# A hand-made issue order built anew: other keys for every step, and three more margins in the planner

## The chip, the cores and the metric

One core of one Trainium2 chip runs the kernel. The metric is the device time of one execution in microseconds (us). TensorE is called PE, its weight loads PEld, VectorE DVE, ScalarE ACT, GpSimd POOL; SyncE (SP) issues nearly all DMAs, and its queue is SPq in the profile.

## What is computed

A causal seven-tap local average with softmax weights, then a two-layer block with SoLU and a normalization in between (cut from the reference):

```python
# x (8, 4160, 192), weight_gen (8, 4160, 8 heads, 7 taps)
w = exp(weight_gen - max); w = w / (sum(w) + 1e-09)
out = einsum('bshk,bskhg->bshg', w, x_unf)        # x_unf: 7 shifted copies of x, zeros ahead
x = out.reshape(33280, 192)
h = x @ w_in                                      # 192 x 1024
e = exp(h - max(h)); sm = e / (sum(e) + 1e-09)
solu = h * sm
ln = (solu - mean) / sqrt(var + 1e-06) * g_ln
return ln @ w_out                                 # 1024 x 192
```

## The kernel before

The 33280 rows are cut into 260 tiles of 128 rows (128 partitions hold runs of 260 consecutive rows; tile t is row t of each run). Sixteen tiles make a chunk (the first two are 4 and 8 tiles), four tiles a group. Numbers are split into two float16 halves ("high" and "low"), so each product is three matmuls with the halves.

The work of a tile is a chain of steps over the five engines. The names in brackets are those of the planner.

- Per chunk: SP loads x in four parts (`lx0` to `lx3`, L87) and the weights (`lw`, L93); seven steps make the softmax of the taps (`t0` to `t6`; `t5` is DVE's reciprocal on L122, `t6` POOL's multiplication on L124); ACT and DVE compute the scale of the chunk (`v0` to `v5`).
- Per group of four tiles: POOL multiplies x by the taps (`attA`, L180) and adds part of the seven products (`attB`, L195). In two groups of four DVE adds the rest (`fin`, L458, tile `a`); in the other two PE adds them while it transposes. POOL has three buffers `pr`.
- Per pair of tiles: PE transposes the pair into PSUM tile `pa` (`xT`, L474: nine matmuls from `pr`, or three from `a`); ACT takes the high half (`xhi`, L484), DVE the low one (`xld`, L488) into `xh`; SP copies 64 partitions of `xh` to the other half of the partitions, both ways, into `turned` (`sw`, L494, two DMAs: the exchange of halves). `xh` and `turned` have four buffers each.
- Per tile: PE's first product (`mm1`, L508 and L513, twelve matmuls into `h`) reads `xh` and `turned`. Then DVE `max` (L525), ACT `exp` (L531), DVE `solu` (L539), ACT `sq` (L545) and `hi` (L552), DVE `lo` (L556). `h` has three buffers, so `mm1` of tile t waits for `sq` and `lo` of tile t - 3. SP transposes both halves by DMA (`tr`, L564) into `hlT` (six buffers, so it waits for `mm2` of tile t - 6). PE's second product (`mm2`, L604, 24 matmuls) follows, then ACT `out` (L615), and once in four tiles SP stores (`od`, L618). Small steps `f0` to `f5` per group make the normalization's scales.

Every engine runs its instructions in the order in which the program gives them. That order is not the source's: `plan` lists each step with its engine, a cost in ns and the steps it follows, and `issue_order` runs a list scheduling over it. When an engine comes free in that model, it takes, of the steps that are ready by then, the one with the smallest key. The key is the tile number plus an entry of the table `URGENCY`; an entry such as `mm1_3` is for that tile alone, `mm1` for all others. `gap` says how long after a step its follower counts as ready; `MARGIN`, looked up by the first two letters of both names, adds nanoseconds to it for tiles above 11. Nothing of the model reaches the chip but the order: on the chip an instruction starts when its inputs are there and the ones ahead of it on its engine have been issued.

```python
key = [round(t + URGENCY.get(f"{name}_{t}", URGENCY.get(name, 0)), 6) for name, t, *_ in steps]
...
    late = MARGIN.get((step[0][:2], to[0][:2]), 0) if to[1] > 11 else 0
...
    name, t, _, cost, *_ = steps[i]
    order.append((name, t))
```

Of the kernel before, what the change touches and what calls it, by code (L numbers as in the profile page):

```python
# [26 lines left out]
def tile_kernel(ctx: ExitStack, tc: tile.TileContext, x, weight_gen, w_in, w_out, g_ln, out):  # L27
# [642 lines left out]


URGENCY = dict(
    a00=71.5, a01=199.3, a02=-74.3, a03=-138.9, a04=-169.6, a10=-89.4, a11=203.9, a12=90.1,
    a13=-52.8, a14=90.6, attA=102.4, attA_0=57.6, attA_2=16.5, attA_4=-68.2, attA_6=-48.8,
    attA_8=83, attB=119.3, attB_0=-211.7, attB_2=5.7, attB_4=41.6, attB_6=-32, attB_8=-5.3,
    b0=239.2, b1=12.3, b2=-212.2, b3=-146.2, b4=171.8, c00=84.4, c01=55, c02=-166.7, c10=20.3,
    c11=135.4, c12=117.8, c20=-32.3, c21=-46.1, c22=-89, c30=95.7, c31=-78.4, c32=-191, dup=57.3,
    dup_0=0.9, dup_2=-49.2, dup_4=18.3, dup_6=109.3, dup_8=-102.8, exp=-176.9, exp_0=75.9,
    exp_1=-2.7, exp_10=179.6, exp_11=-117.4, exp_2=-0.5, exp_3=-46.2, exp_4=-188, exp_5=-32.6,
    exp_6=-150.7, exp_7=-98.5, exp_8=-221.2, exp_9=-48.7, f0=-122.4, f0_1=54.1, f0_11=-81.6,  # L680
    f0_3=79.3, f0_5=-73.5, f0_7=-51.7, f1=-185.9, f1_1=209.6, f1_11=162.5, f1_3=-185.1, f1_5=14.2,
    f1_7=118.9, f2=-25.5, f2_1=140, f2_11=-3.2, f2_3=76.2, f2_5=37.3, f2_7=-21.4, f3=95.6,
    f3_1=142.7, f3_11=86.8, f3_3=-147.3, f3_5=-184.5, f3_7=-139.5, f4=-147.9, f4_1=35.8,
    f4_11=-213.2, f4_3=156.3, f4_5=-57.7, f4_7=162.9, f5=-70.1, f5_1=-10.5, f5_11=-124.5,
    f5_3=-15.6, f5_5=-48.4, f5_7=-152.3, fin=188.2, hi=37.5, hi_0=148.8, hi_1=-28.1, hi_10=-47.9,
    hi_11=52.9, hi_2=45, hi_3=-174.9, hi_4=98.5, hi_5=44.4, hi_6=-12.5, hi_7=-111.8, hi_8=177.4,
    hi_9=0.2, lo=-185.7, lo_0=-96.1, lo_1=168, lo_10=83.3, lo_11=112.6, lo_2=43, lo_3=-9.3,
    lo_4=-94.3, lo_5=-69.3, lo_6=-100.4, lo_7=-194.9, lo_8=231.8, lo_9=-61.3, lw=-84.8, lx0=-101.7,
    lx1=-64.2, lx2=-78.8, lx3=-37.7, max=97.3, max_0=-15.2, max_1=-102.4, max_10=-26.9,
    max_11=-14.8, max_2=-40.5, max_3=-197.3, max_4=18.4, max_5=-82.8, max_6=-206.8, max_7=-49.1,  # L690
    max_8=27.3, max_9=-25.4, mm1=-18.1, mm1_0=-24.2, mm1_1=-1.2, mm1_10=-64.4, mm1_11=-47.7,
    mm1_2=173.8, mm1_3=91.2, mm1_4=31.9, mm1_5=-39.6, mm1_6=-0.8, mm1_7=30.6, mm1_8=27.5765,
    mm1_9=-213.6, mm2=-11.4, mm2_0=-133.1, mm2_1=-31.1, mm2_10=108.3, mm2_11=197.9, mm2_2=-56.1,
    mm2_3=-73.5, mm2_4=85.6, mm2_5=14.1, mm2_6=-97.8, mm2_7=-39.3, mm2_8=18.4, mm2_9=58.5, n0=-90.7,
    n1=-39.4, n2=-116, n3=-82.1, n4=-83.6, n5=-87.1, n6=-56.8, n7=-63, nq=-111.6, od=-162.9,
    od_11=-14.1, od_3=81.1, od_7=-146.5, out=-240.4, out_0=-17.5, out_1=0.12526, out_10=18.9,
    out_11=50.9, out_2=-92.8, out_3=-21.1, out_4=219.7, out_5=-76.7, out_6=-65.5, out_7=36.3,
    out_8=-199.4, out_9=-127.6, p30=-243.7, p31=-6.2, p4=78.6, p5=-112.5, p6=78.6, p70=208.1,
    p71=-151, p80=-114, p81=-169.3, p9=74, q00=-231.7, q01=-7.3, q02=146, q10=-178.8, q11=85,
    q12=-209.5, q20=22.2, q21=4.2, q22=-232.2, q30=151, q31=-39.3, q32=67.5, solu=-164.3,  # L700
    solu_0=-104.7, solu_1=-50.5, solu_10=238.5, solu_11=80.8, solu_2=210.1, solu_3=-56.1,
    solu_4=144.2, solu_5=-5.7, solu_6=103.5, solu_7=193.1, solu_8=96.9, solu_9=-154.4, sq=94.8,
    sq_0=73.6, sq_1=114.8, sq_10=-8.4, sq_11=166.9, sq_2=-191.8, sq_3=100.9, sq_4=79.7, sq_5=-175.5,
    sq_6=87.2, sq_7=231, sq_8=-43.1, sq_9=15.3, sw=-10.8, sw_0=14.2, sw_10=-0.6, sw_2=-85.8,
    sw_4=11.9, sw_6=-101.3, sw_8=-70.3, t0=243.9, t0_0=-146.7, t0_4=187.5, t1=28.4, t1_0=-142.4,
    t1_4=60.2, t2=70.4, t2_0=56.7, t2_4=204.6, t3=189.9, t3_0=148.2, t3_4=-233.9, t4=99.7,
    t4_0=-99.3, t4_4=93.5, t5=226.6, t5_0=84.6, t5_4=103.6, t6=44.7, t6_0=147.6, t6_4=30, tr=124.8,
    tr_0=-73, tr_1=186.1, tr_10=81.7, tr_11=135.8, tr_2=134.6, tr_3=-158.7, tr_4=-171.4, tr_5=89.1,
    tr_6=33.7, tr_7=31, tr_8=148.1, tr_9=-215.3, v00=-156.7, v00_0=-71.2, v00_4=129.8, v01=130.6,
    v01_0=124.8, v01_4=18.5, v02=163.5, v03=89.6, v1=-101.5, v1_0=-175.6, v1_4=62.2, v2=61.2,  # L710
    v2_0=67.1, v2_4=-138.4, v3=193.6, v3_0=86, v3_4=165.3, v4=-59.5, v4_0=-225.6, v4_4=-229.6,
    v5=-1.5, v5_0=59.8, v5_4=56.8, w0=-14.1, w1=-65.5, x0=50, x1=-101.8, xT=-20.7, xT_0=-130.6,
    xT_10=224.8, xT_2=-144.6, xT_4=-175.2, xT_6=-66.3, xT_8=157.5, xhi=-136.6, xhi_0=-227.5,
    xhi_10=238.1, xhi_2=27.4, xhi_4=-213.7, xhi_6=44, xhi_8=-195.5, xld=105.4, xld_0=129.3,
# [211 lines left out]
def held(t):  # L926
# [114 lines left out]
```

## Time and profile before

| | |
|---|---|
| time, median of 3 runs (lowest to highest) | 1304.97 us (1304.77 to 1308.33) |
| the profiled execution: its time | 1307.43 us |
| its span, first to last instruction | 1305.4 us |
| mean granted PE clock | 0.979 |
| busy: PE, DVE, POOL, ACT | 92%, 89%, 88%, 87% |
| HBM read and written | 46.19 MB, 25.56 MB |

No engine is full on average, and four of them are between 87% and 92% busy. The work of 16 tiles repeats from about 146 us to 1142 us; ahead of it the weights are prepared and the pipeline fills, behind it the last tiles drain and no softmax work is left. The stretch from 146.2 to 1141.7 us is 13 such cycles, measured from the first product of tile 20 to that of tile 228. In a cycle PE issues 32 products (16 `mm1` and 16 `mm2`) and eight `xT`.

### The profile page before, as it was taken

What the parts mean: (1) busy time and instruction counts of PE and PEld (TensorE: products, weight loads), DVE (VectorE), ACT (ScalarE), POOL (GpSimd) and SP (SyncE); (2) the same over time, 40 slices, a digit from 0 to 9 for tenths busy, and PEclk for the clock granted to TensorE, in tenths of its full rate; (3) what the DMA queues carried; (4) which work ended last, traced back from release to release, by engine and by line L of the source; (5) the groups of instructions that cost most, each with busy time, mean ns of one, the idle gap of its engine ahead of it and who ended that gap; (6) DMA issues with size and microseconds to landing.
All of it is one profiled execution on the core that took longest, in us unless ns stands there. A gap on an engine that the chain in (4) does not pass through costs nothing.

```text
span 1305.4 us, 27349 instructions
## 1 busy us (share of the span) xinstructions
PE 1206.9 (92%) x10248; PEld 822.9 (63%) x10248; DVE 1157.8 (89%) x1786; ACT 1137.1 (87%) x2311; POOL 1146.7 (88%) x237
## 2 busy tenths in 40 slices
PE   2698999989999998989899999999999999999998
PEld 2364666656666665656666566666666666666666
DVE  6778889979899997989989899999989899999894
ACT  5788979878898988989888898989899898998886
POOL 4999999988989999798997989899899989999700
PEclk9799999989999998999999999999999999999999
DMA  6578688777878878697987979889797989977686
GB/s 211 139 182 181 132 177 173 166 159 151 200 157 193 179 161 179 134 197 157 192 154 149 209 144 200 166 175 184 156 208 143 206 157 183 169 152 127 138 167 128
DMA packets 586066, 219.75 MB, mean 168 GB/s; under 512 B 548687, under 2 KB 566223, under 8 KB 585806
## 3 DMA queue, kind: packets, MB, share of 16 engines
q1 hardware_dynamic: 585632, 216.91, 79.9%
q8 instruction: 80, 1.31, 0.4%
q10 hardware_dynamic: 302, 1.11, 0.3%
q14 instruction: 52, 0.43, 0.1%
HBM read 46.19 MB, written 25.56 MB: 55 GB/s over the span
## 4 chain that ended last, share of the span: by engine, by line
PE 39%; ACT 25%; DVE 17%; issue 10%; DMA 6%; SPq 2%; ACTq 0%; DVEq 0%
PE po L604 15%; PE h L513 13%; PE h L508 7%; ACT e L531 7%; ACT e L545 6%; DVE h L525 5%; DVE h L539 5%; ACT hl L552 5%; DMA turned<-xh 4%; DVE hl L556 3%; PE pa L474 3%; ACT ot L615 2%; DVE a L458 2%; ACT junk L145 2%; ACT xh L484 1%
## 5 line engine op out<-in xcount | busy, mean ns | idle before, releaser
L180 POOL TENSOR_TENSOR pr<-xt,wt 128x5376 f32<-128x5376 f32 (+1 forms) x67 | 631.1, 9419 | 4.6 <-PE pa L474 4.3
L604 PE MATMUL po<-w_hl,hlT 128*128 128x192 f16 x6192 | 557.4, 247 | 4.1 <-ACT ot L615 3.5
L604 PEld LDWEIGHTS <-hlT 128*128 128x128 f16 x6240 | 526.7, 98 | 45.4 <-issue 9.5
L195 POOL TENSOR_TENSOR pr<-pr 128x2304 f32<-128x2304 f32 (+1 forms) x126 | 457.9, 3634 | 8.8
L525 DVE TENSOR_SCALAR_CACHE_REDUCE h<-h,row 128x1024 f32<-128x1024 f32 x260 | 334.8, 1288 | 66.0 <-PE h L513 65.3
L539 DVE SCALAR_TENSOR_TENSOR h<-h,row,e 128x1024 f32<-128x1024 f32 x260 | 334.6, 1287 | 23.0 <-ACT e L531 20.3
L531 ACT ACTIVATE e<-h,stats 128x1024 f32<-128x1024 f32 x260 | 291.6, 1122 | 56.8 <-DVE h L525 54.1
L556 DVE SCALAR_TENSOR_TENSOR hl<-h,hl 128x1024 f16<-128x1024 f32 x260 | 315.8, 1220 | 24.3 <-ACT e L545 16.2
L552 ACT ACTIVATE hl<-h 128x1024 f16<-128x1024 f32 x260 | 266.3, 1025 | 40.7 <-DVE h L539 25.1
L545 ACT ACTIVATE e<-h,stats 128x1024 f32<-128x1024 f32 x260 | 290.5, 1118 | 4.0 <-DVE h L539 1.9
L513 PEld LDWEIGHTS <-xh 128*128 128x128 f16 x1560 | 133.4, 99 | 242.4 <-issue 124.1
L513 PE MATMUL h<-w_odd,xh 128*128 128x512 f16 x780 | 192.6, 383 | 0.0
L513 PE MATMUL h<-wa_hi,xh 128*128 128x512 f16 x520 | 183.8, 395 | 0.0
L508 PE MATMUL h<-wb_hi,turned 64*128 64x512 f16 x260 | 102.4, 394 | 40.2 <-DMA turned<-xh 40.1
L615 ACT ACTIVATE ot<-po,stats 128x192 f32<-128x192 f32 x258 | 109.3, 423 | 14.9 <-PE po L604 14.8
L508 PE MATMUL h<-w_odd,turned 64*128 64x512 f16 x390 | 106.7, 380 | 12.5 <-ACT e L545 8.8
L508 PE MATMUL h<-wb_hi,xh 64*128 64x512 f16 x260 | 101.2, 389 | 12.6 <-DVE stats L576 8.8
L508 PEld LDWEIGHTS <-turned 64*128 64x128 f16 x780 | 55.0, 95 | 89.3 <-DMA turned<-xh 45.9
L508 PE MATMUL h<-w_odd,xh 64*128 64x512 f16 x390 | 106.9, 381 | 0.0
L513 PE MATMUL h<-wa_lo,xh 128*128 128x512 f16 x260 | 102.5, 394 | 0.0
L474 PE MATMUL pa<-ident,pr 128*128 128x128 f32 x678 | 87.1, 276 | 3.5 <-DVE xh L488 3.5
L474 PEld LDWEIGHTS pa<-ident,pr 128*128 128x128 f32 x678 | 79.3, 143 | 15.3 <-issue 3.5
(89 smaller groups left out, 1011.7 us busy)
## 6 DMA issues: line engine op xcount, KB each, us to landing
out_dram<-ot SPq DMA_DIRECT2D x65, 384.0 KB, 3.2
xt<-in_x_dram SPq DMA_DIRECT2D x30, 576.0 KB, 4.8
xt<-in_x_dram SPq DMA_DIRECT2D x30, 480.0 KB, 4.1
turned<-xh SPq DMA_DIRECT2D x260, 32.0 KB, 2.1
wt<-in_weight_gen_dram SPq DMA_DIRECT2D x15, 448.0 KB, 4.7
hlT<-hl SPq DMA_TRANSPOSE x260, 4.6
xt<-in_x_dram SPq DMA_DIRECT2D x3, 384.0 KB, 4.7
pr<-in_moe_w_out_dram SPq DMA_DIRECT2D x1, 1024.0 KB, 10.1
```

Of the source, the lines that this page charges most:

```text
L180: nc.gpsimd.tensor_tensor(out=window(pr, 0, [(ROW, K), (HG, n * H), (1, HG)]), in0=window(xt, t * D, [(D, K), (HG, n * H), (1, HG)]), in1= ...
L195: nc.gpsimd.tensor_tensor(out=b, in0=b, in1=a, op=ALU.add)
L474: nc.tensor.matmul(pa[:, k], source[:, first : first + P], ident, is_transpose=True, start=at == 0, stop=at == 3 * len(sources) - 1,)
L508: nc.tensor.matmul(h[:, fs], last[(f + odd) % 2][rows, low], rhs[rows], start=n == 0, stop=False)
L513: nc.tensor.matmul(h[:, fs], xh[:, 2 * odd, low], rhs[:, fs], start=False, stop=n == 2)
L525: nc.vector.tensor_scalar(h, h, row(t, BACK), 3.0e38, op0=ALU.mult, op1=ALU.min, accum_out=stat(t, NMAX))
L531: nc.scalar.activation(e, h_of[t], AF.Exp, bias=stat(t, NMAX), scale=-1.0, accum_out=stat(t, Z))
L539: nc.vector.scalar_tensor_tensor(out=h, in0=h, scalar=row(t, SCALE), in1=e, op0=ALU.mult, op1=ALU.mult, accum_out=stat(t, M))
L545: nc.scalar.activation(e_of.pop(t), h_of[t], AF.Square, bias=stat(t, M), scale=-float(FF), accum_out=stat(t, Q),)
L552: nc.scalar.activation(hl[:, 0, :], h_of[t], AF.Copy, scale=2.0**14)
L556: nc.vector.scalar_tensor_tensor(out=hl[:, 1, :], in0=h_of[t], scalar=2.0**14, in1=hl[:, 0, :], op0=ALU.mult, op1=ALU.subtract,)
L604: nc.tensor.matmul(po[:, :D], hlT[:, half * NJ + j, :], w2_hl[:, j, w, :], start=n == 0, stop=n == len(terms) - 1,)
```

## The change

Nearly every entry of `URGENCY` has another value, and `MARGIN` has three entries more: `sw` to `mm1` (and any other name with these first letters) 6000 ns, `xld` to `sw` 1500 ns, `mm2` to `tr` 1000 ns. `plan`, the costs, the buffers and the steps themselves stay. Of the table, one line of each side:

```diff
-    b0=239.2, b1=12.3, b2=-212.2, b3=-146.2, b4=171.8, c00=84.4, c01=55, c02=-166.7, c10=20.3,
+    attA=42.9, attA_0=-139.3, attA_2=38.7, attA_4=-121.9, attA_6=101.7, attA_8=-218.2,
...
 MARGIN = {
     ("lx", "v0"): 6000, ("lw", "t0"): 6000, ("lx", "at"): 6000, ("t0", "t1"): 6000,
     ("t1", "t2"): 3000, ("t2", "t3"): 3000, ("t3", "t4"): 3000, ("v2", "t4"): 3000,
-    ("t5", "t6"): 6000,
+    ("t5", "t6"): 6000, ("sw", "mm"): 6000, ("xl", "sw"): 1500, ("mm", "tr"): 1000,
 }
```

**SP, around the store of tiles 140 to 143** (the row `out_0_dram<-ot`). Before, the two exchanges here are those of tiles 152 and 154, and the transposing DMA in the first row is that of tile 146:

```order
L564 DMA_TRANSPOSE hlT_9359<-hl_9334 128x16x128
L564 DMA_TRANSPOSE hlT_9414<-hl_9388 128x16x128
L494 DMA turned_9482<-xh_9454 64x256 x2
L564 DMA_TRANSPOSE hlT_9488<-hl_9462 128x16x128
L618 DMA out_0_dram<-ot_9284 128x768
L564 DMA_TRANSPOSE hlT_9581<-hl_9518 128x16x128
L564 DMA_TRANSPOSE hlT_9605<-hl_9584 128x16x128
L494 DMA turned_9633<-xh_9578 64x256 x2
```

After, around the same store; the first transposing DMA is that of tile 144, and the exchanges are again those of tiles 152 and 154, with that of tile 156 in the last row:

```order
L564 DMA_TRANSPOSE hlT_9269<-hl_9230 128x16x128
L564 DMA_TRANSPOSE hlT_9328<-hl_9302 128x16x128
L494 DMA turned_9331<-xh_9262 64x256 x2
L564 DMA_TRANSPOSE hlT_9380<-hl_9345 128x16x128
L494 DMA turned_9405<-xh_9372 64x256 x2
L564 DMA_TRANSPOSE hlT_9453<-hl_9403 128x16x128
L618 DMA out_0_dram<-ot_9323 128x768
L564 DMA_TRANSPOSE hlT_9538<-hl_9484 128x16x128
L564 DMA_TRANSPOSE hlT_9593<-hl_9560 128x16x128
L87 DMA xt_9600<-in_x_dram 128x960
L93 DMA wt_9615<-in_weight_gen_dram 128x896
L494 DMA turned_9655<-xh_9562 64x256 x2
```

The exchange of tile 152 stood behind the transposing DMA of tile 147 and now stands behind that of tile 145; that of tile 154 moved from behind tile 150's to behind tile 146's.

**DVE, around `fin` of tile 156** (the row L458). Before, it follows the maximum of tile 150:

```order
L488 TENSOR_TENSOR xh_9454<-pa_9416,xh_9454 128x3x128
L556 SCALAR_TENSOR_TENSOR hl_9462<-h_9339,hl_9462 128x1024
L539 SCALAR_TENSOR_TENSOR h_9392,stats_135<-h_9392,row_8248,e_9466 128x1024
L525 TENSOR_SCALAR h_9468,stats_135<-h_9468,row_8248 128x1024
L458 TENSOR_REDUCE a_9521<-pr_9281 128x768
L556 SCALAR_TENSOR_TENSOR hl_9518<-h_9392,hl_9518 128x1024
```

After, it follows the maximum of tile 149 and a small step of the scales:

```order
L525 TENSOR_SCALAR h_9438,stats_135<-h_9438,row_8094 128x1024
L576 TENSOR_REDUCE stats_135<-stats_135 128x4
L458 TENSOR_REDUCE a_9492<-pr_9228 128x768
L556 SCALAR_TENSOR_TENSOR hl_9484<-h_9382,hl_9484 128x1024
L539 SCALAR_TENSOR_TENSOR h_9438,stats_135<-h_9438,row_8094,e_9508 128x1024
```

The addition comes one tile of DVE's work earlier.

**POOL, around `t6` of the chunk that starts at tile 164** (the row L124). Before:

```order
L180 TENSOR_TENSOR pr_11235<-xt_9659,wt_8682 128x5376
L195 TENSOR_TENSOR pr_11235<-pr_11235 128x2304
L195 TENSOR_TENSOR pr_11235<-pr_11235 128x768
L124 TENSOR_TENSOR wt_9661<-wt_9661,wy_10643 128x896
L180 TENSOR_TENSOR pr_11481<-xt_9659,wt_8682 128x5376
```

After:

```order
L180 TENSOR_TENSOR pr_11186<-xt_9600,wt_8636 128x5376
L124 TENSOR_TENSOR wt_9615<-wt_9615,wy_10380 128x896
L195 TENSOR_TENSOR pr_11186<-pr_11186 128x2304
L195 TENSOR_TENSOR pr_11186<-pr_11186 128x768
L180 TENSOR_TENSOR pr_11445<-xt_9600,wt_8636 128x5376
```

The multiplication that reads DVE's reciprocal now stands ahead of the group's additions instead of behind them.

## Rows read from the trace of the kernel before

**Rows 1.** Busy time by stretch: engines in their order, then granted clock, DMA share, GB/s.

```profile
core 0: us, PE busy (x) PEld busy (x) DVE busy (x) ACT busy (x) POOL busy (x), PEclk, DMA share, GB/s
0.00:146.20 146.20, 100.91 (x727) 66.01 (x728) 111.49 (x185) 112.99 (x257) 126.97 (x37) 0.92 0.70 171
146.20:1141.70 995.50, 950.85 (x8137) 647.27 (x8136) 908.82 (x1392) 889.69 (x1796) 931.24 (x184) 0.98 0.84 172
...
842.60:917.70 75.10, 72.06 (x625) 49.31 (x624) 69.81 (x108) 68.31 (x139) 71.60 (x15) 1.00 0.88 177
```

**Rows 2.** What PE waited for from 146.2 to 1141.7: total us, times, longest.

```profile
PE h L508 <- DMA turned<-xh: 36.5, 15, 5.9
PE h L508 <- ACT e L545: 5.8, 13, 0.6
PE h L508 <- DVE hl L556: 1.3, 2, 0.7
PE po L604 <- ACT ot L615: 0.9, 2, 0.7
```

**Rows 3.** The first of these waits over the whole span.

```profile
PE h L508 <- DMA turned<-xh: 40.1, 17, 5.9
```

**Rows 4.** Timeline of one stop, tile 188: start us, us, engine, line, operation.

```profile
946.72 0.55 DVE L488 TENSOR_TENSOR xh<-pa,xh 128x384 f16<-128x384 f32 x1
...
948.81 4.37 SPq L564 DMA_TRANSPOSE hlT<-hl  x1
...
953.28 1.18 SPq L494 DMA_DIRECT2D turned<-xh  x2
...
953.41 0.39 PE L508 MATMUL h<-wb_hi,xh 64*128 64x512 f16 x1
...
956.17 0.39 PE L508 MATMUL h<-wb_hi,turned 64*128 64x512 f16 x1 [2.38 <-DMA turned<-xh]
```

**Rows 5.** All uses of tile `turned`: from a DMA's issue to its landing.

```profile
DMA to landing us min/median/max: 1.7/2.1/6.3
```

**Rows 6.** What POOL waited for from 146.2 to 1141.7.

```profile
POOL wt L124 <- DVE wy L122: 52.6, 12, 7.0
POOL pr L180 <- PE pa L474: 4.3, 1, 4.3
```

**Rows 7.** The same in its four last cycles, 842.6 to 1141.7.

```profile
POOL wt L124 <- DVE wy L122: 12.6, 4, 3.4
```

**Rows 8.** Timeline of POOL around the end of tiles 184's and 180's groups.

```profile
877.13 8.57 POOL L195 TENSOR_TENSOR pr<-pr 128x2304 f32<-128x2304 f32 x2
...
895.43 6.97 POOL L195 TENSOR_TENSOR pr<-pr 128x2304 f32<-128x2304 f32 x2
```

**Rows 9.** Timeline of PE: the transposes of tiles 180 (from `a`) and 184 (from `pr`).

```profile
906.18 0.49 PE L474 MATMUL pa<-ident,a 128*128 128x128 f32 x3
...
923.90 1.15 PE L474 MATMUL pa<-ident,pr 128*128 128x128 f32 x9
```

**Rows 10.** Timeline of DVE: `fin` of tile 180.

```profile
898.16 1.78 DVE L458 TENSOR_REDUCE a<-pr 128x768 f32<-128x1536 f32 x1
```

**Rows 11.** Busy time by stretch again, a slow cycle.

```profile
612.60:691.20 78.60, 74.80 (x627) 50.61 (x628) 69.86 (x108) 68.59 (x139) 71.20 (x14) 0.96 0.86 168
```

More of the change, by code (lines that the diff above doesn't have):

```diff
@@ L672 @@
 URGENCY = dict(
-    a00=71.5, a01=199.3, a02=-74.3, a03=-138.9, a04=-169.6, a10=-89.4, a11=203.9, a12=90.1,
-    a13=-52.8, a14=90.6, attA=102.4, attA_0=57.6, attA_2=16.5, attA_4=-68.2, attA_6=-48.8,
-    attA_8=83, attB=119.3, attB_0=-211.7, attB_2=5.7, attB_4=41.6, attB_6=-32, attB_8=-5.3,
-    b0=239.2, b1=12.3, b2=-212.2, b3=-146.2, b4=171.8, c00=84.4, c01=55, c02=-166.7, c10=20.3,
-    c11=135.4, c12=117.8, c20=-32.3, c21=-46.1, c22=-89, c30=95.7, c31=-78.4, c32=-191, dup=57.3,
-    dup_0=0.9, dup_2=-49.2, dup_4=18.3, dup_6=109.3, dup_8=-102.8, exp=-176.9, exp_0=75.9,
@@ L679 @@
[L679 to L714, printed above, removed]
@@ L715 @@
-    xld_10=-17.8, xld_2=8.82093, xld_4=198.6, xld_6=23.9, xld_8=-2.6,
+    a00=79.1, a01=227.6, a02=-179.6, a03=77, a04=-12.8, a10=2, a11=-93.6, a12=123.9, a13=124.9,
+    a14=-132.6, attA=42.9, attA_0=-139.3, attA_2=38.7, attA_4=-121.9, attA_6=101.7, attA_8=-218.2,
+    attB=39.9, attB_0=-162.5, attB_2=-4.3, attB_4=74.8, attB_6=-6.9, attB_8=38, b0=133.1, b1=124.8,
+    b2=-185.2, b3=24.4, b4=6.5, c00=-95.6, c01=-188.7, c02=-219.3, c10=-222.3, c11=130.7, c12=-70.5,
+    c20=-32.3, c21=-46.1, c22=-89, c30=95.7, c31=-78.4, c32=-191, dup=57.3, dup_0=0.9, dup_2=-49.2,
@@ new lines @@
+    dup_4=18.3, dup_6=109.3, dup_8=-102.8, exp=-62.2, exp_0=-133.3, exp_1=-123.8, exp_10=41,
+    exp_11=-48.7, exp_2=130, exp_3=117.3, exp_4=-23.5, exp_5=-229.6, exp_6=143.2, exp_7=-6.5,
+    exp_8=-204.3, exp_9=-18.4, f0=-44.8, f0_1=204, f0_11=72.8, f0_3=17.5, f0_5=17.9, f0_7=216.7,
+    f1=-76, f1_1=20.8, f1_11=-49, f1_3=225.5, f1_5=239.7, f1_7=-14.9, f2=-157.8, f2_1=-115.4,
+    f2_11=-19.4, f2_3=230.5, f2_5=-82.5, f2_7=-212.3, f3=34.7, f3_1=-22.7, f3_11=-9.5, f3_3=-53.7,
+    f3_5=-121.9, f3_7=-4.3, f4=-58.5, f4_1=167.1, f4_11=69.9, f4_3=-149.7, f4_5=-211.4, f4_7=-100.7,
@@ new lines @@
+    f5=-113, f5_1=-19.9, f5_11=23.1, f5_3=75.1, f5_5=47.8, f5_7=96.3, fin=117.5, hi=-107.7,
+    hi_0=83.5, hi_1=117.9, hi_10=-193.7, hi_11=86.1, hi_2=-36.8, hi_3=165.8, hi_4=-85.5, hi_5=32.6,
+    hi_6=-10, hi_7=-26.8, hi_8=154.8, hi_9=166, lo=-80.2, lo_0=57.7, lo_1=-5.6, lo_10=102.5,
+    lo_11=-17.3765, lo_2=-76.7, lo_3=23.7, lo_4=164.3, lo_5=95.8, lo_6=-169.7, lo_7=50, lo_8=-126.6,
+    lo_9=75, lw=235.7, lx0=-56.1, lx1=92.4, lx2=8.2, lx3=54.9, max=202.4, max_0=-105.2, max_1=98.3,
+    max_10=233.7, max_11=125.3, max_2=-23.8, max_3=200.8, max_4=-205, max_5=-32.1, max_6=149.3,
@@ new lines @@
+    max_7=-60.8, max_8=-133.6, max_9=-98.2, mm1=-25.2, mm1_0=-8.9, mm1_1=-9.6, mm1_10=239.3,
+    mm1_11=96.5, mm1_2=158.9, mm1_3=48.1, mm1_4=130.2, mm1_5=-233.5, mm1_6=-5.2, mm1_7=-0.8,
+    mm1_8=-2.4, mm1_9=50.4, mm2=-18.3, mm2_0=-4.1, mm2_1=-79.4, mm2_10=182.9, mm2_11=-132.6,
+    mm2_2=-211.7, mm2_3=118.1, mm2_4=-93, mm2_5=-224.9, mm2_6=147, mm2_7=10.4, mm2_8=71.6,
+    mm2_9=96.2, n0=-12.3, n1=122.3, n2=213.8, n3=-82.1, n4=-104.5, n5=-87.1, n6=-157.4, n7=-151.2,
+    nq=-111.6, od=-89.4, od_11=20.6, od_3=16.1, od_7=25.3, out=-192.5, out_0=82.9, out_1=-156.2,
@@ new lines @@
+    out_10=54, out_11=-146.8, out_2=232.1, out_3=-56.4, out_4=-28.7, out_5=6.1, out_6=-127.6,
+    out_7=23.7, out_8=-74.6, out_9=81.9, p30=-18.7, p31=-152.9, p4=235.2, p5=33.4, p6=-71.9,
+    p70=197.2, p71=64.7, p80=-220.6, p81=-108.5, p9=116.9, q00=125.4, q01=-132, q02=161.9,
+    q10=219.6, q11=-64, q12=-61.2, q20=206.5, q21=-15.5, q22=-201.1, q30=39.3, q31=0.6, q32=-134.4,
+    solu=125.9, solu_0=20.8, solu_1=-3.5, solu_10=129.7, solu_11=17.6, solu_2=6.1, solu_3=-139.9,
+    solu_4=-75.7, solu_5=-145.2, solu_6=161.6, solu_7=-195.9, solu_8=-29.1, solu_9=37.3, sq=-43.8,
@@ new lines @@
+    sq_0=215.3, sq_1=24.9, sq_10=40.3, sq_11=25.5, sq_2=-12.8, sq_3=-12.2, sq_4=105.1, sq_5=-121,
+    sq_6=213.5, sq_7=195, sq_8=12.2, sq_9=135, sw=-185.3, sw_0=13.8, sw_10=20.2, sw_2=-59.6,
+    sw_4=-155.5, sw_6=-182.2, sw_8=175, t0=212.4, t0_0=-187, t0_4=28.8, t1=140.8, t1_0=-28.9,
+    t1_4=183.2, t2=-37.7, t2_0=-126.3, t2_4=-82.2, t3=-76.5, t3_0=-74.6, t3_4=38.2, t4=-62.6,
+    t4_0=-136.6, t4_4=-54.8, t5=-63.4, t5_0=-21.5, t5_4=76, t6=-177.7, t6_0=-127.1, t6_4=6.6,
+    tr=92.3, tr_0=149.1, tr_1=51.9, tr_10=240.9, tr_11=-11.4, tr_2=116.2, tr_3=181, tr_4=-86.1,
@@ new lines @@
+    tr_5=-53, tr_6=80.2, tr_7=-115.4, tr_8=-93.9, tr_9=-198.8, v00=-59.2, v00_0=115.8, v00_4=5.3,
+    v01=-39.3, v01_0=223.2, v01_4=-36.3, v02=168.3, v03=-45.4, v1=222.8, v1_0=15.8, v1_4=1.3,
+    v2=-79.9, v2_0=202.6, v2_4=206.9, v3=194.4, v3_0=-66.4, v3_4=3.8, v4=47.2, v4_0=49.8,
+    v4_4=-37.3, v5=115.1, v5_0=-200.7, v5_4=75.3, w0=12.4, w1=-58.5, x0=115.8, x1=-0.7, xT=-175.2,
+    xT_0=-80.4, xT_10=-88.9, xT_2=57.7, xT_4=-138, xT_6=-69.7, xT_8=245, xhi=-93.7, xhi_0=-188.9,
+    xhi_10=-138.1, xhi_2=19.7, xhi_4=-3.8, xhi_6=24.9, xhi_8=178.1, xld=249.2, xld_0=-95.4,
@@ L716 @@
+    xld_10=99.8, xld_2=-77.8, xld_4=-238.1, xld_6=8.8, xld_8=133.1,
 )
```

## The prediction

> **What bounds the kernel now.** I read the busy time by stretch first. From 146.2 to 1141.7 us the work of 16 tiles repeats 13 times in 995.5 us, 76.6 us a cycle, and PE is busy for 950.9 us of it, more than any other engine [rows 1]. In a cycle where PE's clock was 1.00 throughout, its work is 72.06 us [rows 1], so 13 cycles need 936.8 us; the other 14.1 us of PE's busy time are time at the lower of its two clock levels (1.2 and 2.4 GHz, the stretch's mean is 0.98). Next I read what PE waited for in this stretch: 36.5 us for `turned`, 5.8 us for ACT's squares, 1.3 us for DVE's low half, 0.9 us for ACT's `out`, 44.5 us in all [rows 2]. Busy time and waits add up to the 995.5 us, so PE is the bound, and 58.6 us (44.5 and 14.1) is all that an order could take from this stretch without shortening PE's work.
>
> The largest wait has one cause that the timeline shows. DVE finished the low half of tile 188 at 947.27 us. SP issued its exchange at 953.28 us: until 953.18 its queue was in a transposing DMA that took 4.37 us to issue. PE had begun that tile's first product at 953.41, and stood until the halves had landed, at 956.17 [rows 4]. So it is the place in SP's queue, not the length of the transfer, that makes PE stop.
>
> **The exchange, part one of the change.** Counted in the written order over tiles 20 to 249, 2.61 products of PE lie on average between an exchange and the product that needs it before, and 8.83 after. A cycle has 32 products, so one stands for 72.06 / 32 = 2.25 us, its share of the transposes included; the lead goes from 5.9 to 19.9 us. The longest stop of PE at `turned` is 5.9 us [rows 3] and a landing takes at most 6.3 us [rows 5]; both together stay below the new lead. I take all 36.5 us of the stretch out, and the 40.1 - 36.5 = 3.6 us ahead of and behind it [rows 2, 3]. With the stops goes what follows them: the lowered clock. Nearly all of PE's waiting is for `turned`, the other waits being at most 0.7 us long [rows 2], so I give it all 14.1 us back. Together **54.2 us**. The exchange itself does the same two DMAs; what moves with it costs nothing as long as SP's queue is not fuller, and it holds the same DMAs as before.
>
> Here a rule of the Trainium skill speaks against any gain. The page "DMA: Bandwidth & Descriptors", section "Anatomy of one DMA — SWDGE (gpsimd) path", gives a fixed cost of about 2.0 us plus the bytes over 436 GB/s, for another issuing path than SP's. By that a copy of 32 KB would take an estimated 2.1 us, the old lead would have covered it, and there would be no wait to remove. The median landing agrees with the page, 2.1 us [rows 5]; the timeline does not agree that the lead was there, since the copy was issued just ahead of the product [rows 4].
>
> **The transposes of x move with it.** To be exchanged earlier a pair has to be transposed earlier: `xT` stands 11.80 products ahead of `mm1` instead of 5.30, that is 6.5 x 2.25 = 14.6 us. Who is late next? POOL finished the group of tile 184 at 902.4 us [rows 8], and PE transposed it at 923.9 [rows 9]: 21.5 us of lead, of which 6.9 remain. In the groups that DVE finishes, POOL was done at 885.7 us [rows 8], and PE transposed at 906.2 [rows 9]; `fin` took 1.78 us of these 20.5 [rows 10], so 20.5 - 1.8 - 14.6 = 4.1 us remain, if DVE takes `fin` up as early as the new order has it (1.48 products ahead of `xT`, before 3.79). Both are covered, so I cost the move at nothing; without that cover each microsecond that POOL or DVE comes later would be one of PE's. A buffer bounds the move too: `xh` and `turned` hold four pairs, and the new order starts a pair 11.80 products, about six tiles, ahead, which leaves one tile. The cast and the subtraction of a pair move along on ACT and DVE; there are as many as before, and what their new places do to the tiles' own steps is in the term of ACT and DVE below.
>
> **The margin ahead of the transposing DMAs, and SP.** `mm2` to `tr` puts these DMAs behind other entries of SP's queue. Between `tr` and its `mm2` there are 7.50 products after and 7.66 before, 0.4 us less. No wait of PE for `hlT` is among [rows 2]; I cost it at nothing.
>
> **The order on ACT and DVE.** This is the term that the trace of before doesn't show, since the keys of all steps are others. The `h` buffers tie PE to it: a product waits for the squares and the low half of the tile three back. These waits were 5.8 + 1.3 = 7.1 us, in 15 places, 0.6 to 0.7 us at the longest [rows 2]. In the written order the squares begin with no other product between them and the product that waits for 29 of 230 tiles before, and for 67 after. The bounds: below, the new order may fit better, and all 7.1 us go; above, each of the 67 costs the longest such wait of ACT, 0.6 us, 40 us, or 33 more than now. I take the waits to grow with the number of tight places, 7.1 x 67 / 29 = 16.4 us, **9.3 us more**; the 15 places where they occurred against 29 tight ones say that a tight place costs little, so the value lies near the lower end.
>
> **The head** (0 to 146.2 us) has another order too. PE is busy for 100.9 us there and its clock is at 0.92 [rows 1]; the margins don't hold for tiles up to 11. I see no sign to either side, and take 0, with 6 us either way, the size of one long stop [rows 3].
>
> **The sum.** 36.5 + 14.1 + 3.6 - 9.3 = 44.9 us less. The profiled execution has a span of 1305.4 us, so 1260.5; its time of 1307.43 us is 2.0 above its span and 2.5 above the median of the runs. I take the gain from the median: 1304.97 - 44.9 = **1260.1 us**. A cycle would then last (995.5 - 36.5 - 14.1 + 9.3) / 13 = 73.4 us.
>
> **Rivals.**
> *POOL becomes the bound.* Without its waits of 52.6 and 4.3 us [rows 6] POOL takes 938.6 us for 13 cycles, 72.2 us each: as much as PE. It waits only for DVE's reciprocal, once a cycle, 12.6 / 4 = 3.15 us in the last four [rows 7]. If that wait stays where it is while PE gets faster, a cycle is 75.35 us, 13 of them 979.6, and the gain is 15.9 + 3.6 = 19.5 us: 1285.5 us. For it: four engines within a few per cent of each other, and POOL's `t6` now stands ahead of a group's additions. Against it: POOL waits there because it has run ahead of PE (21.5 us), and `t5` stands 4.9 products ahead of `t6` instead of 4.3.
>
> *PE stops at the transposes, and the kernel gets slower.* PE takes its instructions in order; an `xT` that waits for POOL or `fin` now holds up some 12 products that have their inputs, where it held up 5. If DVE, full with the maxima, comes to `fin` more than the 4.1 us later than POOL's end allows, PE stops once a cycle for some microseconds and its clock falls as at the other stops. One cycle of before had such a price in full: 78.6 us, with PE busy for 74.8 at a clock of 0.96 [rows 11]. All 13 like that are 1021.8 us, 26.3 more, less the 3.6: 1327.7 us. It decides from (995.5 + 3.6) / 13 = 76.9 us a cycle on, which is 4.8 us of stops and clock above PE's 72.06. Against it: the leads of 6.9 and 4.1 us.
>
> *Nothing changes.* The exchanges come earlier but PE then waits as long for the rings of ACT and DVE. That the lead itself isn't lengthened is excluded by the order. By the page's rule above, too, there is nothing to win here: 1305 us, or with the 9.3 us of the tighter order 1314.3. PE's stops at 36.5 us speak against it.
>
> **How the numbers follow.** The forecast, 1244 to 1275 us: 0.67. POOL as the bound, 1275 to 1299: 0.17. Nothing changes, 1301 to 1315: 0.06, half of it within 0.3%. Slower through the transposes: 0.10. About 0.3%, 3.9 us, is what a measurement of this kernel can tell from no change. Faster: 0.67 + 0.17 = 0.84; same 0.03; slower 0.03 + 0.10 = 0.13. The range begins with the lower bound of the ring (1304.97 - 54.2 - 7.1 = 1243.7) and reaches over most of the POOL case, whose own spread includes the ring's upper bound (1304.97 - 54.2 + 33 = 1283.8) and the head's 6 us: 1244 to 1296.
>
> **What would show it.** In the profile after: no stop of PE for `turned` from 146 us on; a mean granted clock of about 1.00 in the repeating stretch; cycles of 73 to 74 us; POOL's wait at L124 shorter than before; waits of PE for L545 and L556 of some 16 us. A row of PE's transposes (L474) waiting for L195 or L458 would show the slower case; PE waiting for POOL while POOL waits at L124 the case of POOL. I am wrong in kind if the exchanges still stop PE, and wrong in size if the ring's waits are far from 16 us.

## The result, and the profile after

| | before | after |
|---|---|---|
| time, median (lowest to highest), 4 runs each | 1304.87 us (1296.62 to 1308.33) | 1253.26 us (1251.95 to 1254.43) |
| the profiled execution: time, span | 1307.43, 1305.4 us | 1254.43, 1252.4 us |
| mean granted PE clock | 0.979 | 0.989 |

The kernel after takes 0.9613 of the time before (95% interval 0.9567 to 0.9659): 51.6 us less, where 44.9 were forecast.

The busy time by stretch, after, in the columns of [rows 1]. The second row is again the 13 cycles from the first product of tile 20 to that of tile 228, the third one cycle of them:

```profile
0.00:153.30 153.30, 105.75 (x768) 70.74 (x768) 114.93 (x190) 117.35 (x267) 132.52 (x39) 0.91 0.69 166
153.30:1091.00 937.70, 930.44 (x8114) 639.89 (x8112) 907.39 (x1393) 880.22 (x1795) 931.50 (x185) 1.00 0.90 182
...
802.00:874.00 72.00, 71.55 (x626) 49.20 (x624) 69.80 (x109) 67.72 (x139) 71.53 (x15) 1.00 0.91 184
...
1091.00:1252.40 161.40, 152.99 (x1370) 107.70 (x1368) 134.64 (x206) 131.19 (x252) 81.72 (x15) 1.00 0.72 144
```

The 13 cycles went from 995.5 to 937.7 us, 72.1 us each, and PE is busy for 930.44 of the 937.7 us. What PE waited for in this stretch, after (total us, times, longest; it answers to [rows 2]; the row with L556 is `mm1` waiting for `lo`, L545 for `sq`, L615 is `mm2` waiting for `out`):

```profile
PE h L508 <- DVE hl L556: 4.2, 13, 0.5
PE h L508 <- ACT e L545: 0.8, 3, 0.4
PE po L604 <- ACT ot L615: 0.5, 1, 0.5
```

There is no stop for `turned` any more. The balance, profiled run against profiled run:

| part of the span | before | after | difference |
|---|---|---|---|
| 13 cycles: PE waits for `turned` | 36.5 | 0 | -36.5 |
| 13 cycles: PE waits for DVE and ACT | 8.0 | 5.5 | -2.5 |
| 13 cycles: PE busy | 950.85 | 930.44 | -20.4 |
| 13 cycles: PE idle in no row of waits | 0.15 | 1.8 | +1.6 |
| ahead of them (146.2, now 153.3) and behind (163.7, now 161.4) | 309.9 | 314.7 | +4.8 |
| span | 1305.4 | 1252.4 | -53.0 |

The place of an exchange in SP's queue, after, is shown by tile 180. Timeline of DVE, SP and PE from the subtraction to the product (start us, us, engine, line, operation, as in [rows 4]):

```profile
851.60 0.55 DVE L488 TENSOR_TENSOR xh<-pa,xh 128x384 f16<-128x384 f32 x1
...
850.52 6.55 SPq L564 DMA_TRANSPOSE hlT<-hl  x2
857.12 1.23 SPq L494 DMA_DIRECT2D turned<-xh  x2
...
874.03 0.39 PE L508 MATMUL h<-wb_hi,turned 64*128 64x512 f16 x1
```

The subtraction ended at 852.15 us, but SP was inside two transposing DMAs until 857.07. So the exchange still stands behind them, and is 5.0 us late here. What is new is that the product comes at 874.03 us, 15.7 us behind the end of the issue. In [rows 4] a like delay, 6.0 us, ran straight into the product.

Tile 180 is no exception. Over the 104 exchanges of the 13 cycles, the traces give from the end of the subtraction to the start of the issue 0.9 us in the median before and 4.4 us after, and more than 3 us in 30 of them before and in 82 after. The exchanges wait longer in SP's queue than they did; but each one after has landed at least 9.2 us ahead of its product, where 29 before landed less than 1 us ahead. The change gave the exchanges lead and no freer queue.

### The profile page after: what moved, and what is told of

The parts are those of the page before. It is cut to its first block, busy times and chain, and to the rows that moved or that the text cites. A ratio compares the mean times of both kernels' runs of the same rounds, so it can differ in the third digit from the quotient of the medians.

```text
span 1252.4 us, 27348 instructions
## 1 busy us (share of the span) xinstructions
PE 1189.2 (95%) x10248; PEld 818.3 (65%) x10248; DVE 1157.0 (92%) x1786; ACT 1128.8 (90%) x2311; POOL 1145.7 (91%) x237
## 4 chain that ended last, share of the span: by engine, by line
PE 34%; ACT 33%; DVE 17%; issue 11%; DMA 4%; SPq 0%; ACTq 0%; DVEq 0%
PE po L604 13%; PE h L513 11%; ACT e L531 9%; ACT e L545 8%; ACT hl L552 6%; PE h L508 6%; DVE h L539 5%; DVE h L525 4%; DVE a L458 4%; PE pa L474 3%; DVE hl L556 3%; ACT junk L145 3%; ACT ot L615 2%; DMA hlT<-hl 2%; ACT xh L484 2%
## 5 line engine op out<-in xcount | busy, mean ns | idle before, releaser
L556 DVE SCALAR_TENSOR_TENSOR hl<-h,hl 128x1024 f16<-128x1024 f32 x260 | 314.6, 1220 | 41.5 <-ACT e L545 26.4
L545 ACT ACTIVATE e<-h,stats 128x1024 f32<-128x1024 f32 x260 | 292.2, 1124 | 2.6 <-DVE h L539 2.0
L513 PE MATMUL h<-wa_hi,xh 128*128 128x512 f16 x520 | 178.4, 384 | 0.0
L615 ACT ACTIVATE ot<-po,stats 128x192 f32<-128x192 f32 x258 | 110.5, 428 | 36.4 <-PE po L604 36.0
L513 PE MATMUL h<-wa_lo,xh 128*128 128x512 f16 x260 | 99.2, 381 | 0.0
L508 PEld LDWEIGHTS <-xh 64*128 64x128 f16 x780 | 54.7, 94 | 54.8 <-issue 26.0
```

The source lines that it names most:

```text
L508: nc.tensor.matmul(h[:, fs], last[(f + odd) % 2][rows, low], rhs[rows], start=n == 0, stop=False)
L513: nc.tensor.matmul(h[:, fs], xh[:, 2 * odd, low], rhs[:, fs], start=False, stop=n == 2)
L545: nc.scalar.activation(e_of.pop(t), h_of[t], AF.Square, bias=stat(t, M), scale=-float(FF), accum_out=stat(t, Q),)
L556: nc.vector.scalar_tensor_tensor(out=hl[:, 1, :], in0=h_of[t], scalar=2.0**14, in1=hl[:, 0, :], op0=ALU.mult, op1=ALU.subtract,)
```

## Experiments

All ratios are against runs of the kernel before on the same chip, with 95% intervals; these runs had medians from 1306.4 to 1308.0 us. The theory: PE stopped because each exchange was issued too late, behind transposing DMAs in SP's queue; the new order gives the exchange a lead; the clock that fell with the stops comes back. The rivals: the gain is in another part of the new order (head, ACT and DVE); or the lead moves the wait elsewhere, to a ring (buffers used in turn, as the three `h`: a product waits until the steps of the tile three back have left its buffer).

### The new keys without the three margins

```diff
-    ("t5", "t6"): 6000, ("sw", "mm"): 6000, ("xl", "sw"): 1500, ("mm", "tr"): 1000,
+    ("t5", "t6"): 6000,
```

> The new keys with the old margins: the three new entries of the margins are taken out again. Written out, the order is the same as after the change on PE, DVE, ACT and POOL, and differs in 136 of SP's 538 entries: without the margin between the subtraction and the exchange some exchanges stand a place or two earlier in SP's queue (9.31 products of lead on average instead of 8.83). Theory, that the keys alone give the exchange its lead: 1250 to 1257 us, PE still never stops for the turned halves in the repeating stretch. Rival, that the margins do it: most of the gain is lost, 1280 us or more, with stops of PE at the turned halves.

Measured: 1253.54 us (1251.82 to 1255.89), ratio 0.9586 [0.9557, 0.9616]; the kernel after once more, on another chip, as `e11_after_again`: 1251.65 us, 0.9591 [0.9561, 0.9620]. In the 13 cycles without the margins PE has no stop at `turned` either. The margins bring nothing that these runs can tell. The written orders say why: with the new keys the margins from `sw` to `mm1` and from `mm2` to `tr` move no entry at all, and the one from `xld` to `sw` moves entries of SP alone, 136 of 538. The keys had already put the products far enough back (9.31 products of lead without the margins, 8.83 with them).

> The kernel after once more, on the same chip as the splice at tile 8, as the mark for it: 1251 to 1255 us by all theories.

### The margins with the old keys

```diff
-    ("t5", "t6"): 6000,
+    ("t5", "t6"): 6000, ("sw", "mm"): 6000, ("xl", "sw"): 1500, ("mm", "tr"): 1000,
```

> The old keys with the three new margins. The written order then differs from the old one on all engines, the lead of the exchange is 5.15 products instead of 2.61, and the order no longer repeats from one 16 tiles to the next. If the margins by themselves bring the gain: 1250 to 1265 us. Theory, that they bring lead but an order in which ACT and DVE fit worse, as the single key did: fewer stops at the turned halves, more waits for the squares and low halves, 1272 to 1300 us.

Measured: 1307.11 us (1304.04 to 1308.28, 10 runs), ratio 0.9999 [0.9977, 1.0022]: no gain, outside both of the expected ranges. What PE waited for, over the whole span:

```profile
PE po L604 <- ACT ot L615: 35.8, 41, 3.4
PE po L318 <- ACT junk L311: 21.3, 3, 15.4
PE h L508 <- ACT e L545: 12.4, 18, 1.9
PE h L508 <- DVE stats L576: 12.3, 3, 8.8
PE pa L474 <- DVE xh L488: 8.3, 8, 2.5
PE h L508 <- DVE hl L556: 7.5, 15, 1.0
...
PE h L508 <- DMA turned<-xh: 1.9, 1, 1.9
```

The 40.1 us of [rows 3] are down to 1.9. But PE now waits 35.8 us for ACT's `out`, in 41 places, where the kernel before has 3.5 us of that wait over its span. The stops are removed and all of the gain is given back. The margins shift the written order on all engines; that the keys, made for another order, no longer fit is the likely reason, which no run here separates. So the theory is incomplete: a longer lead is not enough.

### One key, and the chain moved by hand

Two more ways to lengthen the lead in the order of before. The first changes one key of the table, that of `xT`:

```diff
-    v5=-1.5, v5_0=59.8, v5_4=56.8, w0=-14.1, w1=-65.5, x0=50, x1=-101.8, xT=-20.7, xT_0=-130.6,
+    v5=-1.5, v5_0=59.8, v5_4=56.8, w0=-14.1, w1=-65.5, x0=50, x1=-101.8, xT=-175.2, xT_0=-130.6,
```

> The kernel before with one number changed: the key of the transposes of x goes from -20.7 to -175.2, as after the change. In the written order the lead of the exchange over its product goes from 2.61 to 9.26 products, and the places where the squares stand right ahead of the waiting product from 29 to 56 of 230. Theory, that the lead is what counts: PE's 36.5 us of stops at the turned halves and the 14 us of lowered clock go, the rest stays within 10 us: 1250 to 1268 us. Rival, that the whole order of ACT and DVE had to be made anew for it: 1285 us or more, with new waits of PE for the squares and the low halves.

Measured: 1284.81 us (1282.12 to 1285.84), ratio 0.9821 [0.9791, 0.9852], above what the theory expected and 0.2 us from the rival's 1285. PE's waits in its 13 cycles (142.5 to 1121.4 us):

```profile
PE h L508 <- DVE hl L556: 14.4, 20, 2.6
PE po L604 <- ACT ot L615: 12.5, 16, 1.4
PE h L508 <- ACT e L545: 11.5, 14, 1.4
```

Again the stops at `turned` are gone, and 38.4 us of short waits for DVE and ACT stand where 8.0 stood. The second keeps the order of before and moves `xT`, `xhi`, `xld` and `sw` one pair earlier, with `fin` right behind the `max` of the tile eight back:

```diff
+    at = {x: n for n, x in enumerate(order)}
+    place = {x: float(n) for x, n in at.items()}
+    for t in range(44, steps[-1][1] - 1, 2):
+        for n, name in enumerate(("xT", "xhi", "xld", "sw")):
+            place[name, t] = at[name, t - 2] if t > 44 else at["xld", 42] + 0.1 * (n + 1)
+        if ("fin", t) in place:
+            place["fin", t] = at["max", t - 8] + 0.5
+            place["attB", t] = min(place["attB", t], place["fin", t] - 0.2)
+    pool = [x for x in order if x[0][:3] in ("att", "t1", "t6")]
+    for x, y in zip(pool[-2::-1], pool[:0:-1]):
+        place[x] = min(place[x], place[y] - 0.001)
+    order.sort(key=place.get)
     return order
```

> The kernel before, its own keys and margins, with the finished order edited: from tile 44 on the transpose, cast, subtraction and exchange of a pair take the places that those of the pair ahead had, and the sums of DVE are put two tiles earlier; all other steps keep their order on every engine. The lead of the exchange becomes 6.18 products instead of 2.61. Theory, that the lead is what counts and the rest of the old order can stay: the stops at the turned halves go from tile 44 on and the time comes to that of the run without the exchange's wait, 1255 to 1270 us. Rival, that moving the chain alone unsettles ACT and DVE as the single key did: 1280 us or more, with the gain given back as waits for the squares, the low halves and the outputs.

Measured: 1373.77 us (1373.58 to 1374.09), ratio 1.0522 [1.0485, 1.0558]: far slower than the kernel before. The rival's range takes it in, but not for the reason that the trace shows. First the largest waits of POOL, DVE and PE over its span, then the timeline of one turn of the loop they make (a bracket gives the idle time before, and who ended it):

```profile
POOL wt L124 <- DVE stats L576: 110.3, 11, 10.4
...
DVE a L458 <- POOL pr L195: 57.5, 12, 5.1
...
PE h L508 <- DVE hl L556: 72.8, 21, 6.0
```

```profile
715.57 1.76 POOL L124 TENSOR_TENSOR wt<-wt,wy 128x896 f32<-128x896 f32 x1 [10.03 <-DVE stats L576]
...
745.37 8.59 POOL L195 TENSOR_TENSOR pr<-pr 128x2304 f32<-128x2304 f32 x2
...
753.98 1.77 DVE L458 TENSOR_REDUCE a<-pr 128x768 f32<-128x1536 f32 x1 [5.11 <-POOL pr L195]
```

POOL stands 10.03 us until DVE's reciprocal for `t6` has come (the row names `stats`, another small step of DVE near it), and from the start of `t6` needs 753.96 - 715.57 = 38.4 us until the sums for `fin` are done. DVE comes to `fin` earlier than that and stands 5.11 us, so its next reciprocal is late again, once a cycle. To test that this is the cause, one number of that edit was changed, `fin` one tile later:

```diff
-            place["fin", t] = at["max", t - 8] + 0.5
+            place["fin", t] = at["max", t - 7] + 0.5
```

> The same edit of the old order as in the lead by hand, but DVE's sums (fin) stand behind the maximum of the seventh tile ahead instead of the eighth, one tile later. In the first edit DVE came to the sum 33.3 us after the reciprocal t5, POOL needed 38.4 us of work between the two, and DVE stood 5.1 us at the sum in each cycle. One tile is 4.5 to 5 us and the tie has to be paid in both directions: if DVE and POOL tied by t5 and fin are the cause of the 1373.8 us, the stops at the sum all but vanish and 1255 to 1285 us remain. Rival, that the earlier transposes and exchanges themselves broke the order: 1340 us or more.

Measured: 1298.73 us (1296.06 to 1301.63, 10 runs), ratio 0.9945 [0.9917, 0.9972]. DVE no longer waits at `fin`, and 75 us of the 1373.77 are gone with one tile's delay of one instruction in every second group. It is still not the 1255 to 1285 us that was expected. PE's waits in 11 cycles of it (300.2 to 1128.4 us):

```profile
PE h L508 <- ACT e L545: 22.7, 33, 1.1
PE h L508 <- DVE hl L556: 14.5, 11, 1.3
PE po L604 <- ACT ot L615: 0.8, 2, 0.5
```

No stop at `turned`, but 37.2 us at the ring of `h`. So in all three kernels that lengthened the lead in another way than the new keys and were free of that loop (the margins, the one key, the second by hand), most of the gain or all of it was given back at the rings.

### What the stops alone cost

The order of before, with the second half of each `mm1` reading `xh` in place of `turned`, so that no product waits for an exchange (this leaves the exchanged halves out of the computation; the DMAs stay):

```diff
-        last = [xh[:, 1], turned_of[pair]]
+        last = [xh[:, 1], xh[:, 1]]
```

> The kernel before in its own order, but the first product reads the halves of x that have not been exchanged in place of the exchanged ones, so PE doesn't wait for the exchange, which is still issued and moved. This leaves the exchange out of the computation. Theory, that the stops at the turned halves and the clock they lower are the whole difference: 40.1 + 14.1 us less, 1245 to 1258 us, cycles of 72 to 73 us. Rival, that the rings of ACT and DVE or POOL's waits take the place of these stops in the old order: 1275 us or more.

Measured: 1261.95 us (1260.22 to 1265.62), ratio 0.9653 [0.9622, 0.9685], a little above the theory's range and far from the rival's. Its 13 cycles by stretch, and PE's waits in them:

```profile
143.30:1101.50 958.20, 934.23 (x8139) 641.87 (x8139) 907.59 (x1392) 888.86 (x1796) 932.40 (x184) 1.00 0.88 179
```

```profile
PE h L508 <- ACT e L545: 14.7, 13, 1.5
PE po L604 <- ACT ot L615: 7.4, 13, 1.5
PE h L508 <- DVE hl L556: 1.3, 2, 0.7
```

With the stops gone and nothing moved, PE's busy time falls from 950.85 to 934.23 us, at a clock of 1.00: the lower clock did come from these stops. The waits for ACT and DVE rise from 8.0 to 23.4 us: the stops had hidden them. That is 46.05 us of gain. On the same chip the new keys gained 1308.0 - 1253.54 = 54.5 us. In the stretch the new order is 958.2 - 937.7 = 20.5 us better than this kernel, 17.9 us of it the rings; its head and tail are 9.2 us longer (314.7 against 305.5).

### The exchange alone, moved in SP's queue

The kernel after, with each exchange put back behind a later transposing DMA (no other engine's order changes):

```diff
+    at = {x: n for n, x in enumerate(order)}
+    place = {x: float(n) for x, n in at.items()}
+    for t in range(20, steps[-1][1] - 1, 2):
+        place["sw", t] = max(place["sw", t], at["tr", t - 4 - t // 2 % 2] + 0.5)
+    order.sort(key=place.get)
     return order
```

> The kernel after, every engine's order kept but SP's: each exchange from tile 20 on is put as far back in SP's queue, counted in transposing DMAs, as it stood in the kernel before (lead 3.47 products instead of 8.83; the transposes, casts and subtractions stay early). Theory, that the place in SP's queue makes PE stop: stops at the turned halves come back in most cycles, 1275 to 1305 us. Rival, that it was the early transposes and the better fit of ACT and DVE: no stops, 1250 to 1260 us.

Measured: 1290.32 us (1286.86 to 1296.09), ratio 0.9881 [0.9840, 0.9922], 37 us above the kernel with the new keys on the same chip. The stretch, PE's waits and POOL's wait in it:

```profile
151.10:1122.70 971.60, 942.11 (x8113) 641.93 (x8112) 911.39 (x1392) 885.13 (x1795) 935.12 (x185) 0.99 0.86 176
```

```profile
PE h L508 <- DMA turned<-xh: 25.3, 18, 4.7
PE h L508 <- DVE hl L556: 3.9, 13, 0.5
...
POOL wt L124 <- DVE wy L122: 30.3, 10, 7.1
```

The stops are back with 25.3 us, and PE's busy time with them, 942.11 instead of 930.44 us. The reverse, in the kernel before: each exchange ahead of the one transposing DMA that stands right in front of it.

```diff
+    at = {x: n for n, x in enumerate(order)}
+    queue = [x for x in order if x[0] in ("sw", "tr")]
+    place = {x: float(n) for x, n in at.items()}
+    for t in range(20, steps[-1][1] - 1, 2):
+        n = queue.index(("sw", t))
+        for x in queue[n - 1 : n]:
+            if x[0] == "tr":
+                place[x] = at["sw", t] + 0.1 + (x[1] - t) / 1000
+    order.sort(key=place.get)
     return order
```

> The kernel before with SP's queue alone edited: from tile 20 on each exchange is put ahead of the entry that stood right in front of it, where that is a transposing DMA. The lead over the product doesn't change in the planner's order, only what the exchange stands behind. Theory, that the exchange is late because SP's queue is held by transposing DMAs (4.37 us in the stop that the timeline showed): the stops at the turned halves fall by at least a third, 1275 to 1297 us. Rival, that the exchange is late because its subtraction is: within 6 us of the kernel before.

Measured: 1281.40 us (1281.24 to 1281.96), ratio 0.9813 [0.9773, 0.9854], inside what was expected. Over its span:

```profile
ACT hl L552 <- DMA hlT<-hl: 15.0, 12, 2.4
```

```profile
PE h L508 <- DMA turned<-xh: 13.2, 10, 3.5
PE h L508 <- ACT e L545: 12.6, 15, 1.5
```

(the second pair of rows from 144.1 to 1117.4 us, its 13 cycles). A third of the stops stays, and ACT, which had 1.8 us of this wait before, now waits for the transposing DMAs that came later. Two edits of SP's queue alone, in opposite directions, move the time by +37 and -26 us: where an exchange stands in this queue, ahead of the product that needs it, is the main cause of the stops.

It is not the whole cause. In the kernel before, 14 of the 15 stops in the 13 cycles had an exchange issued 4.2 to 7.7 us after its subtraction had ended. For the ten stops that stay here that delay is only 0.1 to 2.9 us, but from the first issue to the last landing go 5.2 to 6.9 us. Tile 188 of this kernel, its subtraction, exchange and product:

```profile
921.01 0.55 DVE L488 TENSOR_TENSOR xh<-pa,xh 128x384 f16<-128x384 f32 x1
...
923.66 1.14 SPq L494 DMA_DIRECT2D turned<-xh  x2
924.89 3.85 SPq L564 DMA_TRANSPOSE hlT<-hl  x1
...
928.96 0.39 PE L508 MATMUL h<-wb_hi,turned 64*128 64x512 f16 x1 [0.86 <-DMA turned<-xh]
```

The exchange is issued 2.1 us behind its subtraction, and the product still waits for it 5.3 us later. What made these landings long was not tried.

### The head

The first product of tile 20 is 7.1 us later after. Is the head of the old order better? The order of before up to the first product of tile 16 (in a second kernel, of tile 8), then that of after:

```diff
+def spliced(steps):
+    head, rest = issue_order(steps, HEAD_URGENCY), issue_order(steps)
+    head = head[: head.index(("mm1", 16))]
+    taken = set(head)
+    return head + [x for x in rest if x not in taken]
```

> The order of before up to the first product of tile 16, then the order of after for all steps that are left. In the traces before reaches that product 10 us earlier (122.8 against 132.8 us), but its second products are up to 8 us later at tile 9. If the head of after is really worse: 1243 to 1250 us. If it only has first and second products in another order, so that the work done by 190 us is the same: 1250 to 1260 us.

> The order of before up to the first product of tile 8, then that of after. In the traces before reaches that product 6.7 us earlier (84.9 against 91.6 us) and stands 3 us at the turned halves there. If the part ahead of tile 8 is where after's head loses: 1247 to 1251 us; if it is the part from tile 8 to 16: 1252 to 1256 us.

Measured: 1250.98 us (0.9581 [0.9552, 0.9610]) and 1253.09 us (0.9602 [0.9574, 0.9629]), beside 0.9591 [0.9561, 0.9620] for after. The three intervals lie on each other: the head has no part in the result that these runs can tell, and no kernel here is faster than after by more than that.

## Why the prediction was right, point by point

**The cause, and the 36.5 us.** Right. All stops at `turned` in the stretch are gone, with the exchange's lead as the reason: putting back that lead alone brings 25.3 us of them back. One sentence was too simple: that the place in SP's queue and not the length of the transfer makes PE stop. It holds for the order of before; with the place mended a third of the stops stayed, and there the landing was the longer part.

**The lower clock.** Right in kind, too small. I gave it all 14.1 us back; PE's busy time fell by 20.4. Some 2.6 us of the fall are no clock but 23 matmuls fewer in the window (8137 in [rows 1] and 8114, at 0.115 us each). The 6.3 us that I missed are in the floor: I took 72.06 us [rows 1] for a cycle free of the lower clock, 936.8 us for 13, and 13 cycles after hold 930.44. I had taken one good cycle of a disturbed run as the floor.

**ACT and DVE.** The failed step. I let the rings' waits grow with the number of tight places in the written order (squares with no other product between them and the product that waits for them), 29 to 67, from 7.1 to 16.4 us. They are 5.0 us (4.2 and 0.8), so by my own sign I was wrong in size here. The count says nothing:

| kernel | tight places of 230 | waits for `sq` and `lo` in the stretch |
|---|---|---|
| before | 29 | 7.1 us |
| before, without the exchange's wait | 29 | 16.0 us |
| after | 67 | 5.0 us |
| one key | 56 | 25.9 us |
| by hand, second | 29 | 37.2 us (11 cycles) |

What I did not see: part of the rings' cost in the kernel before was hidden by the stops. Without the stops the old order has 23.4 us of waits for ACT and DVE (`out` included) where it had 8.0, which is 15.4 more; the new order takes 17.9 of these away. So the term of 9.3 us more stands for two effects against each other, both larger than it, and came out as 2.5 us less.

**Ahead of and behind the stretch.** I took 3.6 us out; it became 4.8 us more: 7.1 more ahead of the stretch, which is over the 6 us either way that I gave the head, and 2.3 less behind it. The stops at `turned` are gone here too. Most of the 7.1 is the same work in another place. The head holds 41 matmuls more (768, and 727 in [rows 1]) and 4.84 us more of PE's busy time; the stretch holds 23 fewer, and the part behind it 18 fewer (1370, and before 1388):

```profile
1141.70:1305.40 163.70, 155.13 (x1388) 109.63 (x1386) 137.47 (x211) 134.41 (x261) 88.49 (x18) 1.00 0.72 143
```

In the head after, one wait of PE for DVE's low half is 11.8 us long (four of them, 16.4 us, from 0 to 153.3 us). The kernels with the old head are no faster.

**The price of the lead.** Right that it was covered, and the cover was larger than forecast. Timeline of POOL, DVE and PE, after, for tiles 180 and 184:

```profile
829.79 8.61 POOL L195 TENSOR_TENSOR pr<-pr 128x2304 f32<-128x2304 f32 x2
...
846.23 1.77 DVE L458 TENSOR_REDUCE a<-pr 128x768 f32<-128x1536 f32 x1
...
848.45 0.49 PE L474 MATMUL pa<-ident,a 128*128 128x128 f32 x3
```

```profile
848.14 6.98 POOL L195 TENSOR_TENSOR pr<-pr 128x2304 f32<-128x2304 f32 x2
...
863.70 1.15 PE L474 MATMUL pa<-ident,pr 128*128 128x128 f32 x9
```

From POOL's end to PE's transposes are 863.70 - 855.12 = 8.6 us (forecast 6.9) and, less `fin`, 848.45 - 838.40 - 1.8 = 8.3 us (forecast 4.1). I had missed that the new order puts `t5` and `t6` earlier too: in the written order `t5` stands 37 products ahead of the first `mm1` of its chunk, before 30. That this made the cover larger is likely and was not tried alone.

**POOL as the bound.** Wrong rival, for the reason given against it. POOL has no wait at all in the 13 cycles after, where [rows 6] had 52.6 and 4.3 us, and where the kernel with late exchanges has 30.3 again. In the old order without the exchange's wait, over its 13 cycles, with nothing moved on POOL or DVE, it was

```profile
POOL wt L124 <- DVE wy L122: 18.5, 10, 3.1
```

so most of that wait went with PE's stops: it only let POOL run no further ahead than PE let it. But the rival was right that the two are equally full: POOL is busy for 931.50 of the 937.7 us now, so it has 6 us left, and PE 7. Which of them bounds the kernel after was not tried.

**The slower rival.** It did not happen here, but the mechanism is real: moving the chain by hand made DVE wait for POOL at `fin` and POOL for DVE at `t6`, and cost 5.2%. It came through DVE, which stopped at `fin`, and not through PE's transposes. The written order of after differs from that kernel in that `t5` and `t6` moved along; that this is what keeps it free of the loop was not tried by itself.

**The margins.** I named a margin, `mm2` to `tr`, as what puts the transposing DMAs behind other entries of SP's queue. With the new keys it moves no entry. The exchange's lead is made by the keys; with the margins alone nothing is won, and without them nothing is lost.

**A rule set against the trace.** Landings did not get shorter: their median rose from 2.1 us [rows 5] to 2.6, as the tile's row of after shows.

```profile
DMA to landing us min/median/max: 1.7/2.6/6.4
```

The Trainium skill, "DMA: Bandwidth & Descriptors", section "Anatomy of one DMA — SWDGE (gpsimd) path", gives a fixed cost of about 2.0 us for another issuing path than SP's, from which I had estimated 2.1 us for such a copy and a case without gain. The gain came although the copies land later: what was at stake was when they were issued.

**The sum.** That 44.9 us came near 51.6 is in part luck. In the balance of the profiled executions, 53.0 us, the clock and the waits for ACT and DVE gave 6.3 and 11.8 us more than forecast; the parts ahead and behind gave 8.4 less, and PE's other idle time 1.6 less.

**Open.** How much of the 8.4 us between the kernel without the wait and the new keys is ACT's order and how much DVE's was not separated.

## What to carry to other kernels

When an engine waits for a short DMA, look first at what stands ahead of it in the queue that issues it, and compare the end of its producer with its issue; moving that one entry is a cheap test. When a lead is lengthened, look at every step upstream, as one sum placed a tile too early cost 75 us here, and fit the rings of the other engines again, as waits that were hidden behind the stops come out when these go. Don't judge an order by counting close neighbours in it, nor a planner's margin by its number: compare the written orders, and run them.

## What the runs showed of the hardware

The issue of a transposing DMA holds SP's queue for long and unevenly. All 260 of them, before and then after (ns min/median/max, first and last start in us):

```profile
L564 SPq DMA_TRANSPOSE hlT<-hl x260: 1316/2020/6702, 46.8 to 1294.0; - x130
```

```profile
L564 SPq DMA_TRANSPOSE hlT<-hl x260: 1316/2074/5147, 47.4 to 1241.2; - x130
```

For an exchange that itself takes 1.23 us to issue, two of these in front, 6.55 us together, meant a delay of 5.0 us (tile 180). The spread of the runs got smaller as well: on one chip the kernel before ran from 1298.37 to 1313.85 us (17 runs, 1.2%), the kernel after from 1250.63 to 1252.41 (5 runs, 0.14%).
